# A linear-attention and gated-MLP block on one core: attention features in blocks of two heads instead of four

## The chip, the cores and the metric

The kernel runs on one core of a Trainium2 chip. The metric is the device time of one execution in microseconds (us); lower is better. Engines are named TensorE (PE; its weight loads are PEld), VectorE (DVE), ScalarE (ACT), GpSimd (POOL) and SyncE (SP, which here issues nearly all transfers).

## The reference

One transformer block over 2048 tokens of width 512, all in bf16, with a conditioning vector `c` that gives six vectors of 512 for shift, scale and gate:

```
mod = silu(c) @ w_mod  ->  sa, ca, ga, sb, cb, gb
h = layernorm(x) * (1 + ca) + sa
x = x + ga * A(h)
h = layernorm(x) * (1 + cb) + sb
x = x + gb * B(h)

A(h):  32 heads of 16; q, k, v = h @ wqkv
  pq = q @ w_phi[head];  pk = k @ w_phi[head]                  # 16 x 16 per head
  phi_q = [softmax(pq), softmax(-pq)];  phi_k likewise         # 32 features per head
  kv[f, d] = sum over tokens of phi_k[f] * v[d];  z[f] = sum over tokens of phi_k[f]
  o = (phi_q @ kv) / (phi_q . z + 1e-6);  return o @ wo
B(h):  (sigmoid(h @ w_gate) * (h @ w_up)) @ w_down            # inner width 1376
```

## The kernel before

Tokens lie in 16 tiles of 128. Everything is a task of a graph (`G.add`), with the engine that runs it, what it reads and writes, and the buffers it holds; buffers are taken from small pools, among them the 8 banks of PSUM. A text, `ORDER`, names all tasks in one sequence, and each engine runs its own tasks in that sequence; a name with `@A`, `@D` or `@P` is put on ScalarE, VectorE or GpSimd. So the sequence fixes the program of every engine and every queue, and the times in `G.add` do nothing when the kernel runs.

The stages overlap:

- Start: `warm0` (six matmuls on zeros) and `warm1_0` to `warm1_11` (one each) are matmuls whose results nobody reads. `c1`, `c2`, `c3` make silu(c); `modc...` make the modulation columns. `w_phi` is folded into the q and k weights: `bd` builds a block-diagonal matrix from `w_phi` (L578), `tpw`/`wTc` or `wqT` transpose the weights, `fold`/`foldc` multiply (L675).
- Per tile: `st1`, `rs1`, `nmr1`, `xn1` normalise, `tph` (or a transposing transfer `xT1`) transposes, `hm1` modulates into `h1T`. `K`, `V`, `Q` are projections of four matmuls of 512 columns each.
- Features (`feature_tasks`, L763 and on): `e` takes exp of both signs on ScalarE, `n` sums over the 16 features of a head on VectorE, `r` takes the reciprocal, `phi` multiplies. The 1024 features of a token stand in eight groups of 128. In a group come four heads: the order within is sign, feature, head, with the head innermost.
- `kv` (L279 to L287): for each token tile and group, one matmul with 128 features of the group as weights and the group's four heads' values with a column of ones (4 x 17 = 68 columns) as moving operand, summed over all 16 token tiles in two banks `kvacc`. A head's own sums are then one quarter of the block; `kvn` and `kvz` (L289) multiply by a mask (`mask4`) that zeroes the other heads' parts, into `kvb`.
- Queries: `qe`, `qn`, `qphi` as above, and `pT` transposes the features through a transfer. `num` (L325): four matmuls of 68 columns for each half of the groups, contracting 128 features with `kvb`; `rd` takes the reciprocal of the denominators, `u` multiplies. `oT` transposes the result, `out` multiplies by `wo`, `x1` adds the residual.
- MLP: `st2` to `xnT` and `mod` prepare the second normalised input in chunks of 1, 1, 2, 4, 4, 4 tiles; `g`, `u` with a chunk and block number are the gate and up projections, `tg` tanh, `hm` the product, `y` the down projection, `fin` the residual, `st` the store. For the last 96 rows of the inner width, in chunks of four tiles, the up projection is packed (L452): 64 weight columns a matmul, two of them side by side on the two halves of the output partitions.

In the order, key sums and projections of queries and values are interleaved, and from the numerators on, `g`, `u` and `y` matmuls stand between the attention's.

Of the kernel before, what the change touches and what calls it, by code (L numbers as in the profile page):

```python
# [23 lines left out]
HC = 4 * VC  # L24
# [15 lines left out]
pmem ld_x0b wdz warm0 c1 warm1_0 warm1_1 bd st1_2 st1_3 warm1_2 warm1_3 c2 rs1_2 ld_x0a ld_wk0 warm1_4 tpw0 st1_0 rs1_0 wTc0 st1_1 ld_wk1 rs1_1 c3 xn1_0  # L40
nmr1_1 nmr1_2 ld_x1b st1_6 st1_7 tpw1 tpw3 wTc3 wTc1 tpw2 fold10 foldc10 wTc2 ld_wm00b ld_x1a ld_wm00a tph00 fold11 fold13 rs1_4 foldc13 fold12 foldc12 xn1_3
xn1_2 xn1_1 modc1.0 tph10 tph11 st1_4 tph20 tph01 ld_x2b foldc11 tph22 warm1_5 modc1c0 hm1_11@A nmr1_4 xn1_6 xn1_7 st1_5 rs1_3@P st1_11 st1_10 warm1_6
hm1_20@A hm1_10@A tph21 warm1_7 tph41 tph42 hm1_21 rs1_6@P nmr1_3 tph13 ld_wm01a ld_wm01b modc1.1 hm1_01@A hm1_00@A hm1_41@A tph03 tph23 K2a ld_x2a tph02
modc1c1 st1_8 ld_x3a warm1_8 K1a hm1_23 xn1_5 xn1_4 tph12 nmr1_6 st1_9 hm1_03@A hm1_13@A hm1_02@A ld_wv0 wqT3 xn1_10 xn1_11 rs1_5@P K0a K0b tph31 hm1_42@A
warm1_9 hm1_12@A hm1_22@A tph32 e0.0 K3a tph30 K3b hm1_30@A ld_wmga K1b tph33 warm1_10 tph40 st1_14 st1_15 st1_13 hm1_31@A hm1_32 wqT0 e3.0 wqT1 K2b hm1_40
nmr1_5 rs1_8@P n0.0 nmr1_8 hm1_33 e2.0 V0a V1a fold03 xn1_9 xn1_8 V1b V0b e1.0 n2.0 V2a V2b tph50 hm1_50 warm1_11 xn1_15 xn1_14 n1.0 V3a wqT2 fold00 fold01
tph43 r0.0@A va1 va0 phi0.0 foldc03 fold02 foldc01 foldc02 n3.0 st1_12 foldc00 xT1_10 xT1_11 r2.0 va2@D ld_wmm2 modca.0 modca.1 hm1_60@P hm1_63@P hm1_62@P
# [12 lines left out]
hm0.4 hm0.9 u0.2 u0.0 num6a tg0.5 tg0.0 rd3a u3a u0.5 g0.2 hm0.0 hm0.5 rd6a nmr2_1 qe10.0 tg0.2 oT4 g0.10 u0.10 wd6 hm0.2 g0.3 pT7 tg0.3 u6a g0.6 num6b u0.3  # L60
y0.0 y0.1 rd6b tg0.10 hm0.10 hm0.3 num5a num5b u6b rd5b wd3 wd4 wd5 oT3 oT6 xn2_1 qe13.0 tg0.6 rd5a y0.2 u5b g0.7 tg0.7 out4 u5a oT5 qn11.0 u0.6 u0.7 xnT1
num7a hm0.6 hm0.7 mod13@A mod12@A rd7a x1_4 y0.3 out3 qphi11.1@P qphi11.0@P x1_3 st2_3 out6 mod10@A mod11@A g1.2 tg1.2 g1.1 tg1.1 num7b wd7 u1.3 u1.2 hm1.2
u7a g1.4 u1.1 y0.4 rd7b hm1.1 u1.4 y0.5 tg1.4 hm1.4 g1.0 g1.10 u1.10 g1.3 u7b st2_2 rs2_2 tg1.10 tg1.3 hm1.10 hm1.3 pT11 out5 tg1.0 u1.7 g1.7 x1_6 nmr2_2 u1.0
hm1.0 g1.5 u1.5 x1_5 qn10.0 wd8 y0.6 g1.6 oT7 xn2_2 xn2_3 g1.8 y0.7 Q14 y0.8 wd10 tg1.7 tg1.5 hm1.5 out7 u1.8 u1.6 st2_4 tg1.6 xnT2 xnT3 wd9 x1_7 qphi10.0 Q12
hm1.7 st2_6 mod21@P mod20@P qphi10.1@P y1.0 pT10 tg1.8 mod22@A mod23@A hm1.6 g1.9 y1.1 y1.2 tg1.9 u1.9 y0.9 y1.3 y1.4 g2.5 y0.10 g2.6 st2_5 qe12.0 st2_7 hm1.8
qn9.0 tg2.5 qe14.0 rs2_4 hm1.9 rs2_3 nmr2_4 y1.5 u2.0 g2.1 g2.0 tg2.0 xn2_7@D hm2.0 nmr2_3 fin0 y1.6 g2.2 tg2.2 u2.6 u2.2 hm2.2 u2.1 num11b y1.7 g2.4 rd11b
u11b xn2_6@P xnT7 xnT6 u2.5 tg2.1 xn2_5 qphi9.1@P hm2.1 tg2.6 u2.8 xn2_4 hm2.5 g2.3 num11a rd11a u11a u2.9 qphi9.0@P xnT5 y1.8 xnT4 tg2.4 u2.4 hm2.4 hm2.6
tg2.3 g2.9 u2.3 hm2.3 g2.8 tg2.8 tg2.9 u2.7 mod41@P mod43@P mod32@P mod42@P mod31@P qn13.0 g2.10 hm2.8 g2.7 y1.9 num10a qn8.0 num10b y2.0 y1.10 tg2.7 hm2.7
rd10a hm2.9 qphi8.0@P u2.10 pT9 y2.1 y2.2 y2.3 y2.4 y2.5 qn14.0 num9b rd9b qphi13.0 qphi8.1@P mod30@A mod33@A tg2.10 mod40@A y2.6 y2.7 g3.3 wr qphi13.1@P
tg3.3 oT11 g3.0 u10a rd10b u10b pT8 oT10 hm2.10 qn15.0 g3.8 num9a rd9a u9a u3.0 out11 y2.8 g3.1 y2.9 qphi14.1 fin1 x1_11 u9b u3.3 hm3.3 st1 tg3.8 tg3.0 u3.8  # L70
num8a st2_11 num8b rd8b rd8a u8a pT13 qphi15.0 hm3.8 u8b u3.9 g3.4 u3.2 out10 x1_10 qphi14.0 oT8 oT9 hm3.0 st2_10 y2.10 g3.6 u3.6 qn12.0 rs2_6 out8 tg3.4
# [89 lines left out]
def kernel(  # L161
# [102 lines left out]
    def bank(name, shape=None, dtype=FP32):  # L264
        return Buf("bank", shape or [P, 512], dtype, name)
# [793 lines left out]
```

## Time and profile before

| | us |
|---|---|
| median of 3 runs | 205.52 |
| lowest and highest | 205.25, 206.58 |
| the profiled execution | 205.02 |
| its span, first to last instruction | 203.3 |
| busy: PE, PEld | 194.9, 106.7 |
| busy: DVE, ACT, POOL | 160.6, 105.9, 102.1 |

The profile shows one execution. The end of a matmul is modelled and matmuls overlap, so a row's duration (379 ns for 512 columns) is longer than the distance between two starts; distances of starts tell what a matmul holds. A row of the timeline joins equal instructions that follow each other ("x8") and gives the first start and the stretch they cover. In rows of groups, the columns are line, engine, operation, tiles, rows*columns of the weights, shape and count, then busy us, mean ns of one, and the engine's idle time before them with what ended it. L numbers are lines of the kernel before.

### The profile page before, as it was taken

What the parts mean: (1) busy time and instruction counts of PE and PEld (TensorE: products, weight loads), DVE (VectorE), ACT (ScalarE), POOL (GpSimd) and SP (SyncE); (2) the same over time, 40 slices, a digit from 0 to 9 for tenths busy, and PEclk for the clock granted to TensorE, in tenths of its full rate; (3) what the DMA queues carried; (4) which work ended last, traced back from release to release, by engine and by line L of the source; (5) the groups of instructions that cost most, each with busy time, mean ns of one, the idle gap of its engine ahead of it and who ended that gap; (6) DMA issues with size and microseconds to landing.
All of it is one profiled execution on the core that took longest, in us unless ns stands there. A gap on an engine that the chain in (4) does not pass through costs nothing.

```text
span 203.3 us, 4138 instructions
## 1 busy us (share of the span) xinstructions
PE 194.9 (96%) x1447; PEld 106.7 (52%) x1471; DVE 160.6 (79%) x374; ACT 105.9 (52%) x257; POOL 102.1 (50%) x143
## 2 busy tenths in 40 slices
PE   7789999999999999999999999999999999999993
PEld 2455655555464687668844444444444444444442
DVE  3899999999999999999897797794969844326633
ACT  2799999999978984556451115212113311324100
POOL 4698977789689999767670056230030324000000
PEclk9999999999999999999999999999999999999999
DMA  5999975669952792417637224433112030100111
GB/s 172 331 329 182 233 264 102 123 82 280 400 213 43 146 102 55 94 37 106 125 59 103 51 54 103 101 83 77 26 26 69 13 79 31 40 13 7 50 55 55
DMA packets 49453, 22.94 MB, mean 113 GB/s; under 512 B 38065, under 2 KB 47634, under 8 KB 49426
## 3 DMA queue, kind: packets, MB, share of 16 engines
q1 hardware_dynamic: 48896, 22.59, 48.6%
q8 instruction: 13, 0.21, 0.4%
q14 instruction: 14, 0.11, 0.2%
q10 hardware_dynamic: 530, 0.02, 0.1%
HBM read 11.58 MB, written 2.10 MB: 67 GB/s over the span
## 4 chain that ended last, share of the span: by engine, by line
PE 75%; DVE 8%; ACT 4%; DMA 4%; issue 4%; POOL 3%; SPq 0%; POOLq 0%; DVEq 0%
PE y_ps L485 19%; PE u_ps L447 18%; PE g_ps L447 17%; PE a_ps L356 5%; DMA wmod_sb<-in_w_mod_dram 4%; PE k_ps L817 3%; PE warm L600 3%; DVE ks L780 3%; PE num L326 2%; POOL phi L787 2%; PE q_ps L871 2%; PE v_ps L821 2%; PE g_ps L449 1%; ACT h1T L751 1%; DVE qks L780 1%
## 5 line engine op out<-in xcount | busy, mean ns | idle before, releaser
L457 ACT ACTIVATE tg<-g_ps 128x512 bf16<-128x512 f32 (+5 forms) x66 | 28.8, 455 | 66.7 <-PE g_ps L447 39.5
L468 DVE SCALAR_TENSOR_TENSOR wmod_sb<-tg,u_ps 128x512 bf16<-128x512 bf16 (+4 forms) x63 | 30.3, 492 | 18.0 <-ACT tg L457 11.3
L485 PE MATMUL y_ps<-wd_sb,wmod_sb 128*128 128x512 bf16 (+4 forms) x180 | 44.2, 366 | 0.2
L447 PEld LDWEIGHTS <-wg_sb 128*128 128x128 bf16 (+1 forms) x252 | 21.9, 99 | 16.1 <-issue 0.2
L447 PEld LDWEIGHTS <-wu_sb 128*128 128x128 bf16 (+1 forms) x252 | 21.8, 99 | 16.0 <-issue 0.3
L784 POOL TENSOR_TENSOR qphi<-qe,qks 128x512 bf16<-128x512 bf16 x24 | 25.1, 1063 | 3.9 <-DMA pT<-qphi 1.0
L485 PEld LDWEIGHTS <-wmod_sb 128*128 128x128 bf16 (+1 forms) x187 | 17.1, 98 | 16.0 <-issue 0.6
L447 PE MATMUL u_ps<-wT_sb,wu_sb 128*128 128x512 bf16 (+2 forms) x124 | 23.8, 322 | 0.1
L447 PE MATMUL g_ps<-wT_sb,wg_sb 128*128 128x512 bf16 (+2 forms) x122 | 23.0, 321 | 0.2
L447 PE MATMUL g_ps<-wqk_sb,wg_sb 128*128 128x128 bf16 (+4 forms) x127 | 19.9, 286 | 0.1
L447 PE MATMUL u_ps<-wqk_sb,wu_sb 128*128 128x128 bf16 (+4 forms) x127 | 19.8, 286 | 0.2
L492 DVE TENSOR_TENSOR ot<-y_ps,x 128x512 bf16<-128x512 f32 (+2 forms) x17 | 11.1, 654 | 10.5 <-PE y_ps L485 10.4
L780 DVE TENSOR_REDUCE qks<-qe 128x64 bf16<-128x1024 bf16 x16 | 19.2, 1204 | 0.0
L780 DVE TENSOR_REDUCE ks<-e 128x64 f32<-128x1024 bf16 (+2 forms) x22 | 19.1, 905 | 0.0
L376 POOL TENSOR_SCALAR ve<-mv 128x2 f32<-128x2 f32 (+1 forms) x8 | 1.8, 226 | 34.2 <-DVE mv L366 34.1
L776 ACT ACTIVATE e<-k_ps 128x512 bf16<-128x512 f32 (+2 forms) x44 | 17.7, 504 | 0.1
L776 ACT ACTIVATE qe<-q_ps 128x512 bf16<-128x512 f32 x32 | 17.3, 608 | 0.8 <-POOL phi L787 0.4
L787 POOL TENSOR_TENSOR phi<-e,kr 128x1024 bf16<-128x1024 bf16 (+2 forms) x10 | 14.5, 1454 | 3.9 <-ACT kr L795 2.1
L817 PE MATMUL k_ps<-wqk_f,h1T 128*128 128x512 bf16 x61 | 15.9, 379 | 0.1
L356 PE MATMUL a_ps<-wo_sb,oT 128*128 128x512 bf16 x60 | 15.9, 379 | 0.2
L871 PE MATMUL q_ps<-wqk_f,h1T 128*128 128x512 bf16 x60 | 15.7, 379 | 0.2
L821 PE MATMUL v_ps<-wv_sb,h1T 128*128 128x512 bf16 x62 | 15.5, 379 | 0.0
(131 smaller groups left out, 306.4 us busy)
## 6 DMA issues: line engine op xcount, KB each, us to landing
out_dram<-ot SPq DMA_DIRECT2D x15, 128.0 KB, 1.8
x_sb<-in_A_x_dram SPq DMA_DIRECT2D x6, 256.0 KB, 4.9
wmod_sb<-in_w_mod_dram SPq DMA_DIRECT2D x1, 1536.0 KB, 7.4
wu_sb<-in_B_w_up_dram SPq DMA_DIRECT2D x1, 1376.0 KB, 11.0
wg_sb<-in_B_w_gate_dram SPq DMA_DIRECT2D x1, 1376.0 KB, 10.4
wd_sb<-in_B_w_down_dram SPq DMA_DIRECT2D x1, 1280.0 KB, 8.0
wmod_sb<-in_w_mod_dram SPq DMA_DIRECT2D x4, 256.0 KB, 6.0
wqk_sb<-in_A_wqkv_dram SPq DMA_DIRECT2D x2, 256.0 KB, 4.5
```

The costliest lines, as they stand in the source:

```text
L356: pe.matmul(ap_[:], lhsT=oT[:, j, :], rhs=wo_sb[:, j, :], start=(j == 0), stop=(j == KT - 1))
L447: pe.matmul(ps[:fsz, 0:n], lhsT=w[:, j, ft * P:ft * P + fsz], rhs=h[:, j, 0:n], start=(j == 0), stop=(j == KT - 1))
L457: G.add(f"tg{k}.{ft}", {"ACT": 0.13 + n * 0.00083}, lambda e, tg=tg, g_ps=g_ps, fsz=fsz, n=n: act.activation(tg[:fsz, 0:n], g_ps[:fsz, 0:n ...
L468: dve.scalar_tensor_tensor(hm_all[:fsz, hm[k].slot, ft, 0:n], tg[:fsz, 0:n], 1.0, u_ps[:fsz, 0:n], op0=ALU.add, op1=ALU.mult)
L485: mm = pe.matmul(y[:, 0:c1 - c0], lhsT=hm_all[:fsz, hm[k].slot, ft, tl * P:(tl + 1) * P], rhs=wd_sb[:fsz, ft, c0:c1], start=(ft == 0), sto ...
L776: act.activation(ee[:, a:b, s].rearrange("p g f h -> p g (f h)"), kp[:, a * 64:b * 64].rearrange("p (g n) -> p g n", n=64), ACT.Exp, scale ...
L780: dve.tensor_reduce(ks[:, a:b].rearrange("p g s h -> p (g s) h"), ee[:, a:b].rearrange("p g s f h -> p (g s) h f"), axis=AX.X, op=ALU.add)
L784: engine(e).tensor_tensor(ph[:].rearrange("p (g s f h) -> p g s f h", s=2, f=DH, h=4)[:, :, s], ee[:, :, s], ks[:, :, 1 - s].unsqueeze(2). ...
L787: engine(e).tensor_tensor(ph[:, a * P:b * P].rearrange("p (g f h) -> p g f h", f=DH, h=4), ee[:, a:b].rearrange("p g s f h -> p (g s) f h" ...
L817: pe.matmul(kp[:], lhsT=h1T[:, j, t * P:(t + 1) * P], rhs=wqk_f[:, j, D:2 * D], start=(j == 0), stop=(j == KT - 1))
L821: pe.matmul(vp[:], lhsT=h1T[:, j, t * P:(t + 1) * P], rhs=wv_sb[:, j, :], start=(j == 0), stop=(j == KT - 1))
L871: pe.matmul(qp[:], lhsT=h1T[:, j, t * P:(t + 1) * P], rhs=wqk_f[:, j, 0:D], start=(j == 0), stop=(j == KT - 1))
```

## The change

The features' layout is changed from blocks of four heads to blocks of two. A group of 128 features now holds two blocks of 64 (two heads each), each with order sign, feature, head.

- Key sums: for each group two matmuls instead of one, each with 64 weight columns and 2 x 17 = 34 moving columns, into the upper and lower 64 partitions of the same bank columns.
- Numerators: for each group two matmuls, each with 64 of the 128 rows as contraction and 34 columns, into two different banks. One task `num` now makes both halves of a tile (16 matmuls) before either `rd` may begin; a half is now every second pair of heads instead of the first or last 16 heads.
- `kvb`, `mask4` and the masking steps are half as wide; `bd` is built in four instructions instead of two; exp, sums and products of the features have innermost runs of two heads.
- `ORDER` is another sequence altogether, with other places for loads, fillers and engines.

```
-HC = 4 * VC
+HC = 2 * VC
...
-                    pe.matmul(acc[g // 4][:, (g % 4) * HC:(g % 4 + 1) * HC], lhsT=ph[:, g * P:(g + 1) * P],
-                              rhs=vaug[va.slot][:, 4 * g:4 * g + 4, :].rearrange("p h d -> p (h d)"),
-                              start=(t == 0 and g % 4 == 0), stop=(t == NT - 1), skip_group_check=True)
+                    for x in range(2):
+                        pe.matmul(acc[g // 4][64 * x:64 * x + 64, (g % 4) * HC:(g % 4 + 1) * HC], lhsT=ph[:, g * P + 64 * x:g * P + 64 * x + 64],
+                                  rhs=vaug[va.slot][:, 4 * g + 2 * x:4 * g + 2 * x + 2, :].rearrange("p h d -> p (h d)"),
+                                  start=(t == 0 and g % 4 == 0), stop=(t == NT - 1), skip_group_check=True)
...
                 dve.tensor_tensor(kvb[:, 4 * i:4 * i + 4, :].rearrange("p g (h c) -> p g h c", c=VC)[:, :, :, 0:DH],
-                                  src[:, 0:4 * HC].rearrange("p (g h c) -> p g h c", h=4, c=VC)[:, :, :, 0:DH],
-                                  mask4[:].unsqueeze(1).unsqueeze(3).to_broadcast([P, 4, 4, DH]), op=ALU.mult)
+                                  src[:, 0:4 * HC].rearrange("p (g h c) -> p g h c", h=2, c=VC)[:, :, :, 0:DH],
+                                  mask4[:].unsqueeze(1).unsqueeze(3).to_broadcast([P, 4, 2, DH]), op=ALU.mult)
...
+                nps = [bank("num") for _ in range(2)]
+
+                def f_num(e, t=t, nps=nps):
+                    for g in range(NG):
+                        for x in range(2):
+                            pe.matmul(nps[x][:, g * HC:(g + 1) * HC], lhsT=pT[t][64 * x:64 * x + 64, g, :], rhs=kvb[64 * x:64 * x + 64, g, :], start=True, stop=True)
...
-                        for g in range(4):
-                            pe.matmul(ps[:, g * HC:(g + 1) * HC], lhsT=pT[t][:, 4 * i + g, :], rhs=kvb[:, 4 * i + g, :], start=True, stop=True)
...
                     def f_u(e, i=i, ps=ps, den=den, o=o):
-                        dve.tensor_tensor(o[:, 256 * i:256 * i + 256].rearrange("p (g h d) -> p g h d", h=4, d=DH),
+                        dve.tensor_tensor(o[:].rearrange("p (g x h d) -> p g x h d", x=2, h=2, d=DH)[:, :, i],
...
-        for g in range(2):
-            pool.tensor_tensor(bd[:, :, 64 * g:64 * g + 64].rearrange("p k (f h) -> p k f h", h=4), wp_sb[:].unsqueeze(3).to_broadcast([P, KT, DH, 4]),
+        for g in range(4):
+            pool.tensor_tensor(bd[:, :, 32 * g:32 * g + 32].rearrange("p k (f h) -> p k f h", h=2), wp_sb[:].unsqueeze(3).to_broadcast([P, KT, DH, 2]),
...
-        ee = Buf("r2k", [P, NG, 2, DH, 4], BF16, q + "e")
+        ee = Buf("r2k", [P, 2 * NG, 2, DH, 2], BF16, q + "e")
...
-                    engine(e).tensor_tensor(ph[:, a * P:b * P].rearrange("p (g f h) -> p g f h", f=DH, h=4), ee[:, a:b].rearrange("p g s f h -> p (g s) f h"),
-                                            kr[:, a:b].rearrange("p g s h -> p (g s) h").unsqueeze(2).to_broadcast([P, 2 * (b - a), DH, 4]), op=ALU.mult)
+                    engine(e).tensor_tensor(ph[:, a * P:b * P].rearrange("p (g f h) -> p g f h", f=DH, h=2), ee[:, 2 * a:2 * b].rearrange("p g s f h -> p (g s) f h"),
+                                            kr[:, 2 * a:2 * b].rearrange("p g s h -> p (g s) h").unsqueeze(2).to_broadcast([P, 4 * (b - a), DH, 2]), op=ALU.mult)
```

The new order begins as below; then the stretches with the last key sums and the first numerators (`num8a` stands for both halves of tile 8).

```
+wdz warm0 pmem c1 warm1_0 warm1_1 ld_x0b c2 st1_2 st1_3 rs1_2@P ld_x0a ld_wk1 ld_x1a ld_wk0 tpw3 wTc3 st1_1 rs1_1 tpw2 bd ld_x1b ld_wm00b ld_wm00a tpw1 wTc2
+wTc1 c3 nmr1_2 st1_0 xn1_2@A st1_5 xn1_3 rs1_0@P st1_4 st1_7 nmr1_1 ld_x2b xn1_0 st1_6 fold13 fold12 tpw0 wTc0 tph21 fold11 rs1_3@P xn1_1 modc1.0 rs1_4@P
...
+r11.6 V12 V11 K13 warm1_7 K12 ld_wd ld_wg0 grb ld_wu0 r14.0 n11.4 va10 e15.4 va11 mask4 r11.4 n10.0 n15.0 phi11.2@D kv8.0 r10.0@A phi11.4@D warm1_8 kv9.0
+warm1_9 V14 e13.4 e13.0 phi10.0@D n13.4 phi11.6 wo1 e12.0 phi11.0 n13.0 phi14.0 kv10.0 V15 kv11.4 phi14.4@D r13.4@A phi13.4 va14 Q6 V13 Q5 r13.0@A phi13.0
+n12.0 n15.4 r15.0 r15.4 va12 r12.0@A qe6.0 phi12.0@D kv11.6 kv11.0 kv11.2 phi15.0@D warm1_10 phi15.4 va13 qn6.0 Q3 va15 kv12.0 kv13.4 kv13.0 kv14.0 kv15.0
+kv14.4 kv15.4 Q7 kvn0 kvz0 qe3.0 wo0 wo3 wo2 kvz1 kvn1 qphi6.1@P warm1_11 ld_wd2 num0a qphi6.0@P qn3.0 qe5.0 rd0a num2a num1a Q8 rd0b u0a u0b tpo0 qe7.0 rd2a
```

More of the change, by code (lines that the diff above doesn't have):

```diff
@@ L44 @@
[L44 to L47, printed above, removed]
@@ L186 @@
     bmask = cst.tile([P, P], BF16, name="bmask")
-    mask4 = cst.tile([P, 4], BF16, name="mask4")
+    mask4 = cst.tile([P, 2], BF16, name="mask4")
     modc = cst.tile([P, 16], FP32, name="modc")
@@ L589, in f_mask @@
     def f_mask(e):
-        with nc.allow_low_precision(reason="sums of one 1 and 31 zeros"):
-            dve.tensor_reduce(mask4[:], ident[:].rearrange("p (f h) -> p h f", h=4), axis=AX.X, op=ALU.add)
+        with nc.allow_low_precision(reason="sums of one 1 and 63 zeros"):
+            dve.tensor_reduce(mask4[:], ident[:].rearrange("p (f h) -> p h f", h=2), axis=AX.X, op=ALU.add)
     G.add("mask4", {"DVE": 0.2}, f_mask, w=["mask4"])
```

118 lines of the change are left out of this document (57 added, 61 removed).

## The prediction

> **What bounds the kernel now.** I read the page first (busy time by engine, slices, chain), then the busy time by stage, then single matmuls in the timeline of TensorE.
>
> ```profile
> PE 194.9 (96%) x1447; PEld 106.7 (52%) x1471; DVE 160.6 (79%) x374; ACT 105.9 (52%) x257; POOL 102.1 (50%) x143
> PE   7789999999999999999999999999999999999993
> PE 75%; DVE 8%; ACT 4%; DMA 4%; issue 4%; POOL 3%; SPq 0%; POOLq 0%; DVEq 0%
> ...
> core 0: us, PE busy (x) PEld busy (x) DVE busy (x) ACT busy (x) POOL busy (x), PEclk, DMA share, GB/s
> 0.00:15.00 15.00, 11.76 (x103) 6.31 (x105) 10.95 (x36) 10.22 (x29) 9.91 (x31) 1.00 0.95 277
> 15.00:30.00 15.00, 14.62 (x143) 8.44 (x144) 14.59 (x33) 14.84 (x37) 12.95 (x20) 1.00 1.10 235
> 30.00:58.00 28.00, 27.79 (x251) 15.18 (x253) 27.19 (x50) 26.73 (x78) 21.96 (x21) 1.00 0.78 209
> 58.00:70.00 12.00, 11.39 (x104) 6.48 (x103) 11.82 (x33) 10.35 (x22) 11.84 (x12) 1.00 0.38 83
> 70.00:130.00 60.00, 59.56 (x507) 37.92 (x514) 52.95 (x137) 27.72 (x67) 36.37 (x47) 1.00 0.50 84
> 130.00:200.00 70.00, 69.63 (x357) 32.38 (x362) 42.76 (x89) 16.08 (x28) 9.11 (x16) 1.00 0.18 45
> ```
>
> The reader is to see that TensorE has no room left. From 15 us to 200 us it idles 0.38 + 0.21 + 0.61 + 0.44 + 0.37 = 2.0 us in all; the only large hole is the start. The chain gives VectorE 8% of the span, but where it does so TensorE stays full beside it, with value and query projections that nobody needs yet (27.79 of 28 us between 30 and 58 us). So work added to TensorE after 15 us moves the end almost one for one, and at most those 2.0 us can swallow any of it. The profiled execution took 205.02 us (span 203.3 us and 1.7 us around it); the runs shown have a median of 205.52 us, 0.5 us above it. The sum is made against 205.0, and 0.5 is added at the end.
>
> **The price of the small matmuls.** The change touches two groups:
>
> ```profile
> L326 PE MATMUL num<-kvb,pT 128*128 128x68 bf16 x128 | 8.0, 194 | 0.4 <-DVE kvb L299 0.4
> L282 PE MATMUL kvacc<-vaug,phi 128*128 128x68 bf16 x128 | 6.0, 194 | 0.1
> ...
> 32.27 0.42 PE L282 MATMUL kvacc<-vaug,phi 128*128 128x68 bf16 x8
> 32.53 0.27 PE L744 MATMUL tp_h<-ident,xn 128*128 128x128 bf16 x2
> ...
> 10.30 0.55 PE L630 MATMUL modc_ps<-sc_bf,wmod_sb 128*128 128x1 bf16 x16
> L630 PE MATMUL modc_ps<-sc_bf,wmod_sb 128*128 128x1 bf16 x32 | 1.1, 164 | 0.0
> ```
>
> Eight key-sum matmuls of one token tile hold TensorE from 32.27 to 32.53: 0.26 us, 32 ns each. (Durations overlap, so only starts count.) Numerators have the same shape. 256 such matmuls: 32 x 0.26 = 8.3 us. What can halving the columns give? Sixteen matmuls with one single column take 0.55 us, and without the last one's 0.164 us that is 0.386 / 15 = 26 ns each. So one full-array matmul with its own weight load hardly gets below 26 ns at any width, and 68 columns already stand at 32. A gain can come only from two half-array matmuls running side by side.
>
> Column tiles of 64 already stand in this kernel (the packed up-projection, L452), so their pairs have rows:
>
> ```profile
> 128.38 0.38 PE L485 MATMUL y_ps<-wd_sb,wmod_sb 128*128 128x512 bf16 x1
> 128.69 0.30 PE L452 MATMUL u_ps<-wT_sb,wu_sb 128*64 128x256 bf16 x2
> ...
> 128.69 0.63 PE L452 MATMUL u_ps<-wT_sb,wu_sb 128*64 128x256 bf16 x8
> 129.25 0.39 PE L485 MATMUL y_ps<-wd_sb,wmod_sb 128*128 128x512 bf16 x1
> 129.47 0.81 PE L449 MATMUL g_ps<-wT_sb,wr_sb 128*128 128x512 bf16 x3
> ...
> 91.21 0.60 PE L447 MATMUL u_ps<-wqk_sb,wu_sb 128*128 128x256 bf16 x4
> 91.65 0.60 PE L447 MATMUL g_ps<-wqk_sb,wg_sb 128*128 128x256 bf16 x4
> ...
> 128.68 0.14 PEld L452 LDWEIGHTS <-wu_sb 128*64 128x64 bf16 x4 [0.43 <-issue]
> L452 PEld LDWEIGHTS <-wu_sb 128*64 128x64 bf16 x24 | 1.1, 109 | 1.3 <-issue 1.3
> ```
>
> Two packed matmuls of 256 columns together take 0.30 us, about one's duration, so a pair does run side by side. But the visit costs. From the y matmul at 128.38 to the g matmul at 129.47 are 1.09 us. In it lie two 512-column matmuls (129.47 - 129.25 = 0.22 each) and four pairs of 256 columns (91.21 to 91.65: 0.44 for four). 1.09 - 0.44 - 0.44 leaves **0.21 us per visit**: 128.38 to 128.69 is 0.31 where 0.22 is usual (0.09 on the way in), and 128.69 to 129.25 is 0.56 where four pairs need 0.44 (0.12 on the way out). The weight loads stop too ("0.43 <-issue"). I call this the toll of a visit: it looks as if the array ran empty before its tiling is changed, once on either side.
>
> **How many visits.** In the new order, TensorE's tasks between which no other form stands are, for the key sums: 0; 1 and 2; 3; 4; 5; 6; 7; 8; 9; 10; first part of 11; its other parts; 12 to 15 together: **13 visits**. For the numerators: 0, 2, 1 together; 4; 3; 6 and 5; 7; 11; 10; 8; 9; 15; 14; 13; 12: **13 visits**. Key sums never stand next to numerators. Before, all of these were full-array matmuls, without a toll.
>
> Toll: 26 x 0.21 = **+5.5 us**. For row tiles (numerators) the nearest row is the tiny K = 1 product at the start, still at the slow clock:
>
> ```profile
> 3.92 0.26 PE L569 MATMUL c_ps<-ones,c_row 1*128 1x1 bf16 x4
> 4.11 2.31 PE L600 MATMUL warm<-wd_sb 128*128 128x512 bf16 x5
> L569 PE MATMUL c_ps<-ones,c_row 1*128 1x1 bf16 x4 | 0.3, 165 | 0.0
> ```
>
> The last of the four starts at 3.92 + 0.26 - 0.165 = 4.02, the next full matmul at 4.11: 0.09 us instead of 0.03, so at least 0.06 us on the way out. Bounds for a row visit: 0.06 and 0.21; I take 0.21, since a column visit is nearest in size and clock. At the low end 13 x 0.15 = 2.0 us less. The Trainium skill, TensorEngine Tiling (Array Packing), Key Properties, says that changing the tiling mode, not just the tile, drains TensorE; by that rule row tiles pay like column tiles, 5.5 us in all, where the K = 1 row alone would allow 3.5.
>
> Pairs: four weight loads of 64 columns span 0.14 us and one takes 0.109, so the second pair starts 0.03 us behind the first. A pair of 34 columns streams in less (0.11 us for 256 columns is 0.43 ns a column: 15 ns), so the load sets it: 0.03 us, eight pairs 0.24 us against 0.26. 32 x 0.02 = **-0.6 us**. Bounds: 17 ns a pair, were loads hidden (256 x 0.017 = 4.4, a gain of 3.9); 52 ns, were each of the two to need the 26 ns of the single-column row (13.3, a loss of 5.0). I stay at the load row, which has the very shape of the key sums.
>
> **The other edits.** Masking of the key sums halves in elements:
>
> ```profile
> L294 DVE TENSOR_TENSOR kvb<-kvacc,mask 128x256 bf16<-128x256 f32 x2 | 0.8, 423 | 0.0
> L580 POOL TENSOR_TENSOR bd<-wp_sb,bmask 128x256 bf16<-128x256 bf16 x2 | 1.5, 770 | 2.1 <-DMA wp_sb<-in_A_w_phi_dram 2.1
> 14.78 0.38 PE L600 MATMUL warm<-wd_sb 128*128 128x512 bf16 x1
> ...
> 22.31 0.38 PE L600 MATMUL warm<-wd_sb 128*128 128x512 bf16 x1
> 7.53 0.40 PE L679 MATMUL fold_ps<-bd,wT_sb 128*128 128x128 bf16 x4
> 14.20 0.38 PE L817 MATMUL k_ps<-wqk_f,h1T 128*128 128x512 bf16 x1
> L787 DVE TENSOR_TENSOR phi<-e,kr 128x1024 bf16<-128x1024 bf16 x7 | 4.7, 682 | 0.3 <-POOL h1T L753 0.3
> ```
>
> The two masking steps lose at most half of 0.423 us each, 0.3 us of VectorE together, which TensorE's own lateness hides: 0. Reciprocals, products and feature steps keep their counts and elements; only their innermost runs get shorter, from 4 elements to 2. Bounds: 0, and for the feature products on VectorE twice their time, of which the seven key products here are 4.7 us. They run at 0.67 ns an element with runs of 4, quicker than any step that goes element by element (the mask, 423 / 256 = 1.65 ns), so two elements at a time are enough for them; I take 0. The reciprocal of a tile's first half waits for sixteen numerator matmuls instead of four, about 0.12 us a tile, under the gate and up matmuls: 0; uncovered it would be 16 x 0.12 = 1.9 us.
>
> Fillers: both orders hold the 18 "warm" matmuls. In the old one four start after the first key projection at 14.20, from 14.78 to 22.31; in the new order nine do (warm1_3 to warm1_11, five of them among the last key sums). Five more at 0.22 us, where TensorE is full: **+1.1 us**; 0 if TensorE happens to wait there.
>
> Start: bd becomes four instructions on GpSimd, between 1.5 us (by elements) and 3.1 us (by instructions); I take 2.0. It now also stands behind rs1_2. The folds need it, and the first fold started at 7.53 in a stretch where TensorE was waiting anyway for the modulation weights (10.30). Of the 0.5 to 2.5 us that it is later, I let 0.4 us reach the first key projection: **+0.4 us** (0 to 1.5). SyncE's queue keeps its eight leading loads, in another order among them: 0. But the value weights (wv0) now stand behind the transposing loads wqT2 and wqT3:
>
> ```profile
> 9.42 1.01 SPq L551 DMA_DIRECT2D wv_sb<-in_A_wqkv_dram  x1
> 10.47 1.78 SPq L669 DMA_TRANSPOSE wT_sb<-in_A_wqkv_dram  x1
> wv_sb<-in_A_wqkv_dram SPq DMA_DIRECT2D x1, 512.0 KB, 7.0
> 19.38 1.03 PE L821 MATMUL v_ps<-wv_sb,h1T 128*128 128x512 bf16 x4
> ```
>
> Each of the two holds the queue for 1.78 us: 9.42 + 3.6 = 13.0, and 7.0 us to landing make 20.0. The new order has the first value projection behind those of the keys of five tiles (K1 to K4 and K0, 0.86 us each), so at about 14.6 + 4.3 = 18.9 and the transposes between them: 0, at most 0.6.
>
> Sum: 5.5 - 0.6 + 1.1 + 0.4 = 6.4 us. Of the 2.0 us of idle time I let 0.5 be filled by it: 5.9 us. 205.0 + 5.9 + 0.5 = **211.4 us**.
>
> **Rivals.** (a) The two halves do not run side by side when they are so short: 52 ns a pair, 22 ns over my 30: 256 x 0.022 = 5.6 us, 217.0. For it: no row shows a pair this short, and 26 ns was what a single column took. Against it: the packed loads start in pairs. Chance 0.12. The Trainium skill, TensorEngine Tiling (Array Packing), Instruction Overhead, gives each matmul about 60 cycles however few its columns, and warns against taking the tiling factor from a dimension that is already small; the 26 ns row agrees with the floor, and by that rule this rival is the rule rather than the exception.
>
> (b) TensorE stays at half its clock through the start. The fillers of the first 6 us start 0.43 us apart (five from 4.11 until 6.24, when the key weights' transposes follow) and later matmuls of that width 0.22; the new order puts two instead of five behind c1, so TensorE stands idle from about 5.0 until the key weights land at 6.2. If the fast clock then comes only after another 4.7 us of dense work, half of that is lost: +2.3 us, 213.7. For it: the fast clock came only after 5 us without a gap. Against it: the start has holes that may hide it. Chance 0.12.
>
> (c) The tolls vanish in holes: the new order leaves TensorE waiting for VectorE toward the end of the key sums, where five fillers now stand, and the tolls fall into that wait. For it: VectorE is as full as TensorE there (27.19 of 28). Half of the tolls, the fillers and the later start hidden: 211.4 - 2.8 - 1.1 - 0.4 = 207.1; with the cheap row visits (2.0 less) 205.1. Against it: the window has 0.21 us of idle time on TensorE, and the tolls of thirteen visits put TensorE behind VectorE. Chance 0.12.
>
> (d) Faster: the visits are free, because a matmul of 34 columns leaves so little in the array that emptying it costs nothing, and the pairs stream at 17 ns with their loads hidden. The place is every visit, the price 205.5 - 3.9 + 1.1 + 0.4 = 203.1 us; it decides from a toll below 0.015 us a visit, since 26 of that use up what lies between 203.1 and 203.5. For it: the pair row, side by side. Against it: the K = 1 row, where single columns still pay 0.06 us on the way out. Chance 0.06.
>
> **How the numbers follow.** The forecast, 211.4, has 0.58, with 209.4 to 213 as its own range (cheap row visits below; above, the rest of the start's 1.5 us and the 0.5 of idle time left unfilled). About 1% (2 us) is what a measurement of this kernel tells from no change. Slower by over 1%: forecast, (a) and (b), 0.58 + 0.12 + 0.12 = 0.82. Within 1%: (c), 0.12. Faster by over 1%: (d), 0.06. The range 207.0 to 217.5 holds the forecast, (a), (b) and the upper end of (c), and leaves out (d) and the rest of (c).
>
> **What would show it.** In the changed profile: kvacc groups as 128*64 and num groups as 64*128, x256 each, pairs starting within some ns and 0.03 us apart; gaps of about 0.1 us in the starts on both sides of every visit; TensorE still full from 15 us on, the numerators beginning 3 to 4 us later than at 58.57; fillers between 45 and 62 us. Wrong would be: pairs 0.05 us apart (a), 427 ns matmuls after 7 us (b), TensorE idle by several us before the first numerators (c), or starts without gaps around the visits (d).

## The result: 212.3 us, 3% slower, and the profile after

The changed kernel takes 212.26 us (median of 4 runs, 211.67 to 212.38) against 205.38 us of the kernel before beside it: a ratio of 1.0305, 95% interval 1.0264 to 1.0345. The prediction was 211.4 us, range 207.0 to 217.5.

The page of the changed kernel: its span, its busy times and the granted clock of TensorE by slices of a fortieth:

```profile
span 209.8 us, 4656 instructions
PE 199.9 (95%) x1699; PEld 106.7 (51%) x1727; DVE 163.1 (78%) x383; ACT 107.5 (51%) x250; POOL 99.8 (48%) x140
...
PEclk9859999999999999999999999999999999999999
```

Its busy time by stage (the columns are those of the prediction's table; PEclk is the third figure from the end):

```profile
0.00:15.00 15.00, 10.95 (x94) 6.50 (x96) 10.66 (x36) 8.86 (x22) 11.34 (x38) 0.78 0.99 249
15.00:30.00 15.00, 14.68 (x125) 8.18 (x126) 14.46 (x36) 14.80 (x36) 13.20 (x16) 0.99 0.99 257
30.00:60.00 30.00, 29.68 (x343) 14.95 (x343) 28.10 (x48) 27.77 (x78) 21.90 (x21) 1.00 0.74 203
60.00:73.00 13.00, 12.49 (x186) 6.67 (x189) 11.63 (x32) 10.16 (x20) 11.36 (x11) 1.00 0.40 61
```

TensorE is as full as before from 15 us on; the span is 6.5 us longer. The numerators begin at 63.28 us, 4.7 us later than in the kernel before. New is the clock: 0.78 in the first 15 us, where the kernel before had 1.00. PEclk has to be read with care here, since it counts the time until the clock first comes up as full speed. In the kernel before, the first 128-column transposes still start 107 ns apart and only from 6.9 us on 56 ns apart, though PEclk says 1.00 for all of it. From then on that kernel keeps the fast clock; the changed kernel has it from 5.0 us, but runs at half speed again from 8.5 to 15.3 us.

The groups of the two tiled matmuls in the changed kernel:

```profile
L282 PE MATMUL kvacc<-vaug,phi 128*64 128x34 bf16 x256 | 6.3, 185 | 0.0
L325 PE MATMUL num<-kvb,pT 64*128 64x34 bf16 x256 | 5.4, 175 | 0.0
```

One visit of each in the timeline (start, length, operation, shape and count):

```profile
33.33 0.38 PE L819 MATMUL k_ps<-wqk_f,h1T 128*128 128x512 bf16 x1
33.64 0.24 PE L282 MATMUL kvacc<-vaug,phi 128*64 128x34 bf16 x4
33.64 0.43 PE L282 MATMUL kvacc<-vaug,phi 128*64 128x34 bf16 x16
34.00 0.61 PE L819 MATMUL k_ps<-wqk_f,h1T 128*128 128x512 bf16 x2
...
112.63 0.38 PE L487 MATMUL y_ps<-wd_sb,wmod_sb 128*128 128x512 bf16 x1
112.95 0.37 PE L325 MATMUL num<-kvb,pT 64*128 64x34 bf16 x16
113.25 0.82 PE L449 MATMUL u_ps<-wT_sb,wu_sb 128*128 128x512 bf16 x2
```

A visit of the key sums: from the last full matmul's start at 33.33 to the next full one at 34.00 are 0.67 us; less the 0.22 us of a 512-column matmul, TensorE is held for 0.45 us, where the same eight groups took 0.26 us before (0.455 and 0.257 in the unrounded starts). On the way in stand 0.31 instead of 0.22 (0.09 us lost). Sixteen matmuls span 0.43 us with the last one's 0.185: 0.43 - 0.185 = 0.245 for seven pairs and a second partner, 0.03 us a pair and a little more. That leaves 0.45 - 0.245 - 0.09 = 0.115 us on the way out. A visit of the numerators: 112.63 to 113.25 is 0.62, less 0.22 is 0.40 us; in it 0.32 - 0.22 = 0.10 on the way in, 0.37 - 0.175 = 0.195 for the sixteen (25 to 27 ns a pair) and 0.105 out.

So pairs do run side by side, as short as they are. A visit of one tile costs 0.20 us more than before for key sums (0.455 against 0.257) and 0.14 us for numerators (0.394 against 0.257). The expectations below were written with 0.21 and 0.15. Each further tile in the same visit takes 0.25 us for key sums, as before, and 0.20 instead of 0.25 us for numerators, so that a visit of the numerators of two tiles is 0.08 us dearer than with full-array matmuls (0.594 against 0.511) and one of three tiles 0.03 us (0.797 against 0.767).

### The profile page after: what moved, and what is told of

The parts are those of the page before. It is cut to its first block, busy times and chain, and to the rows that moved or that the text cites. A ratio compares the mean times of both kernels' runs of the same rounds, so it can differ in the third digit from the quotient of the medians.

```text
span 209.8 us, 4656 instructions
## 1 busy us (share of the span) xinstructions
PE 199.9 (95%) x1699; PEld 106.7 (51%) x1727; DVE 163.1 (78%) x383; ACT 107.5 (51%) x250; POOL 99.8 (48%) x140
## 4 chain that ended last, share of the span: by engine, by line
PE 88%; DVE 5%; POOL 2%; DMA 1%; issue 1%; ACT 1%; POOLq 0%
PE y_ps L487 18%; PE g_ps L449 17%; PE u_ps L449 17%; PE v_ps L823 7%; PE k_ps L819 6%; PE a_ps L358 5%; PE q_ps L873 5%; PE kvacc L282 3%; PE tp_h L746 2%; PE num L325 2%; DMA x_sb<-in_A_x_dram 1%; PE warm L602 1%; PE g_ps L451 1%; DVE st L704 1%; PE modc_ps L618 1%
## 5 line engine op out<-in xcount | busy, mean ns | idle before, releaser
L459 ACT ACTIVATE tg<-g_ps 128x512 bf16<-128x512 f32 (+4 forms) x66 | 29.1, 456 | 66.2 <-PE g_ps L449 47.2
L487 PE MATMUL y_ps<-wd_sb,wmod_sb 128*128 128x512 bf16 (+4 forms) x184 | 44.8, 366 | 0.2 <-issue 0.2
L449 PEld LDWEIGHTS <-wg_sb 128*128 128x128 bf16 (+1 forms) x252 | 21.4, 99 | 16.5 <-issue 1.2
L449 PEld LDWEIGHTS <-wu_sb 128*128 128x128 bf16 (+1 forms) x252 | 21.4, 99 | 15.6 <-issue 0.4
L786 POOL TENSOR_TENSOR qphi<-qe,qks 128x512 bf16<-128x512 bf16 x23 | 24.0, 1062 | 9.0 <-DVE qks L782 7.2
L487 PEld LDWEIGHTS <-wmod_sb 128*128 128x128 bf16 (+1 forms) x187 | 17.6, 98 | 18.9 <-DVE wmod_sb L470 0.3
L449 PE MATMUL u_ps<-wT_sb,wu_sb 128*128 128x512 bf16 (+2 forms) x120 | 23.0, 321 | 0.2
L789 POOL TENSOR_TENSOR phi<-e,kr 128x1024 bf16<-128x1024 bf16 (+2 forms) x12 | 17.1, 1428 | 7.0 <-DVE phi L789 4.2
L449 PE MATMUL g_ps<-wqk_sb,wg_sb 128*128 128x128 bf16 (+4 forms) x127 | 19.3, 287 | 0.2
L823 PE MATMUL v_ps<-wv_sb,h1T 128*128 128x512 bf16 x60 | 16.0, 380 | 0.2
L873 PE MATMUL q_ps<-wqk_f,h1T 128*128 128x512 bf16 x57 | 15.6, 379 | 0.3
```

Source lines behind the costliest of these rows:

```text
L449: pe.matmul(ps[:fsz, 0:n], lhsT=w[:, j, ft * P:ft * P + fsz], rhs=h[:, j, 0:n], start=(j == 0), stop=(j == KT - 1))
L459: G.add(f"tg{k}.{ft}", {"ACT": 0.13 + n * 0.00083}, lambda e, tg=tg, g_ps=g_ps, fsz=fsz, n=n: act.activation(tg[:fsz, 0:n], g_ps[:fsz, 0:n ...
L487: mm = pe.matmul(y[:, 0:c1 - c0], lhsT=hm_all[:fsz, hm[k].slot, ft, tl * P:(tl + 1) * P], rhs=wd_sb[:fsz, ft, c0:c1], start=(ft == 0), sto ...
L786: engine(e).tensor_tensor(ph[:].rearrange("p (g s f h) -> p g s f h", s=2, f=DH, h=2)[:, :, s], ee[:, :, s], ks[:, :, 1 - s].unsqueeze(2). ...
L789: engine(e).tensor_tensor(ph[:, a * P:b * P].rearrange("p (g f h) -> p g f h", f=DH, h=2), ee[:, 2 * a:2 * b].rearrange("p g s f h -> p (g ...
L823: pe.matmul(vp[:], lhsT=h1T[:, j, t * P:(t + 1) * P], rhs=wv_sb[:, j, :], start=(j == 0), stop=(j == KT - 1))
```

## Experiments

**The order alone.** The new `ORDER` put into the kernel before; each numerator's second half behind its first:

```
-num0a qphi6.0@P qn3.0 ...
+num0a num0b qphi6.0@P qn3.0 ...
```

> The kernel before, with its features in blocks of four heads and full-array key sums and numerators, but with the new order (each numerator's second half stands right behind its first). Theory T (the visits to the tiled mode cost 0.21 us for key sums and 0.15 us for numerators, the late fillers 1.1 us): the 26 visits, 4.4 us, are gone and the fillers stay, 207.9 us. Rival O (the new order costs it all): about 212. Rival L (the layout's other edits cost it: shorter runs on VectorE, GpSimd and ScalarE): about 205.5.

Measured: 209.93 us (208.43 to 210.91), ratio 1.0197 (1.0114 to 1.028). Without one tiled matmul more than before, the new order alone loses more than half of the difference. That was 2 us over theory T and well over rival L. The busy time by stage of this run, with PEclk the third figure from the end:

```profile
7.00:15.00 8.00, 6.75 (x74) 5.26 (x75) 7.30 (x24) 6.82 (x19) 7.66 (x14) 0.53 1.16 281
15.00:18.00 3.00, 3.00 (x15) 1.55 (x14) 2.04 (x8) 1.87 (x5) 2.45 (x5) 0.55 1.18 324
18.00:30.00 12.00, 11.95 (x96) 6.60 (x94) 11.54 (x24) 11.94 (x29) 10.30 (x12) 1.00 0.95 240
```

TensorE ran at half its clock from about 7 to 17.7 us, into the first key projections. In the changed kernel's own profile it was 8.5 to 15.3 us. Its key sums of tile 10 also wait 0.53 us for VectorE's features, which they do not in the changed kernel.

**The start with fillers.** The same kernel, five late fillers out, ten put into the holes of the start (here with "warm" for the renumbered names):

```
-c1 warm1_0 warm1_1 ld_x0b ... tpw2 bd ... fold12 tpw0 wTc0 tph21 ... modc1.0 ...
+c1 warm1_0 warm1_1 warm warm warm ld_x0b ... tpw2 warm warm warm warm bd ... fold12 warm tpw0 wTc0 tph21 warm ... modc1.0 warm ...
...
-K13 warm1_7 K12 ... kv8.0 ... warm1_8 kv9.0 warm1_9 ... warm1_10 ... warm1_11
+K13 K12 ... kv8.0 ... kv9.0 ...
```

> The new order with full-array matmuls (as in the run with the order alone, 209.9 us), the five late fillers taken out and ten put into the holes of the start: three behind the two after c1, four behind the second transpose of the key weights, one each behind the second fold, the first tile's transposes and the first modulation product. Theory K (the start runs at half clock until 15 to 17.7 us since TensorE has holes there): fast clock from about 7 us on, 1.5 to 2.5 us less, 207.5 to 208.4. If the start's clock does not matter: 209.5 to 209.9.

Measured: 206.33 us (206.00 to 206.78, 10 runs), ratio 1.0026 (1.0004 to 1.0049). That is 3.6 us less than the order alone, more than theory K had asked for. The clock in the same windows:

```profile
7.00:15.00 8.00, 6.75 (x90) 4.46 (x88) 7.66 (x25) 7.54 (x21) 7.61 (x15) 1.00 1.19 281
15.00:18.00 3.00, 3.00 (x20) 1.43 (x18) 2.93 (x9) 3.00 (x8) 2.73 (x5) 1.00 1.17 324
```

The two profiles show where it went: 1.7 us up to the first key sums (30.91 against 29.18 us), 1.5 us from there to the first numerator, where the five late fillers stood, and 0.6 us after it. So the clock of the start is about half of the 3.6 us, not all of it. What is left of the new order, 206.3 against 205.7 us, is small. The spread also fell from 2.5 us to 0.8 us. That a run's time depends on when its clock comes up would fit this, but it is not shown: only one run of each kernel has a profile.

**The changed kernel with that start.** The same edit in the changed kernel; taking out the filler between tiles 8 and 9 joins two visits of key sums:

```
-... kv8.0 ... warm1_8 kv9.0 ...
+... kv8.0 ... kv9.0 ...
 (and the start as in the run above)
```

> The changed kernel with the fillers of the run with the new order and a warm start: five late ones out, ten into the holes of the start. 12 visits of key sums, 13 of numerators. Theory T (tolls one for one on top of the same order): 206.3 + 12 x 0.21 + 13 x 0.15 = 210.8 us. Rival W (part of the tolls falls into waits of this order, as the 2.3 us between the order alone and the changed kernel suggest): 208.7. Rival L (the layout's other edits cost as well): over 211.5.

Measured: 210.34 us (209.87 to 210.63), ratio 1.0225 (1.019 to 1.0261): 1.9 us less than the changed kernel, and **4.0 us over the same order and start with full-array matmuls**. Both profiles show a clock of 1.00 from 7 us on. The two visits that were shown above for the changed kernel, in the run with full-array matmuls, the new order and the warm start:

```profile
32.21 0.59 PE L817 MATMUL k_ps<-wqk_f,h1T 128*128 128x512 bf16 x2
32.64 0.42 PE L282 MATMUL kvacc<-vaug,phi 128*128 128x68 bf16 x8
32.90 0.59 PE L817 MATMUL k_ps<-wqk_f,h1T 128*128 128x512 bf16 x2
...
108.47 0.38 PE L485 MATMUL y_ps<-wd_sb,wmod_sb 128*128 128x512 bf16 x1
108.69 0.42 PE L326 MATMUL num<-kvb,pT 128*128 128x68 bf16 x8
108.94 0.59 PE L447 MATMUL u_ps<-wT_sb,wu_sb 128*128 128x512 bf16 x2
```

With the starts of both profiles, the 12 visits of key sums cost 0.198 us more each, eleven visits of numerators 0.137 each, and the two with two and three tiles 0.08 and 0.03: 2.4 + 1.5 + 0.1 = 4.0 us. The tolls arrive whole, and the 4.5 us that the expectation counted were 0.5 too many. Theory T holds, and rival L has nothing left to explain. The 2.3 us between the order alone and the changed kernel were less than 4.0 because the order alone lost 1.2 us more before its first key sums (30.91 against 29.75 us), and, as rival W has it, because a wait ahead of the key sums of tile 10 took up about 0.5.

**Key sums put off, so that fewer visits remain.** On top of that kernel:

```
-kv0.0 ... kv1.0 kv2.0
+kv0.0 kv1.0 kv2.0
(likewise kv6.0 before kv7.0, kv8.0 before kv9.0, kv11.4 before kv11.6)
```

> The changed kernel with the warm start (210.3 us) and only the key sums put off (tile 0's to 1's, 6's to 7's, 8's to 9's, the first part of 11's to the others), the numerators where they were: 9 visits of key sums instead of 12, 13 of numerators. Theory T: 3 x 0.21 = 0.6 us less, and up to 0.8 more less if the wait of 0.78 us before tile 10's key sums goes with them, as it went in the run with all visits merged: 209.7 to 208.9. If merging gains nothing or the matmuls alone set the price: 210.3 or more.

Measured: 208.94 us (208.54 to 210.36), ratio 1.0186 (1.0116 to 1.0256): 1.4 us less, of which 0.6 are three tolls and the rest the wait ahead of tile 10. The intervals of the two ratios overlap, so this rests on the two profiles: the visits of key sums, with the waits ahead of them, hold TensorE for 1.4 us less. The kernel with the warm start, then the one with fewer visits:

```profile
53.25 0.38 PE L823 MATMUL v_ps<-wv_sb,h1T 128*128 128x512 bf16 x1
54.34 0.43 PE L282 MATMUL kvacc<-vaug,phi 128*64 128x34 bf16 x16 [0.71 <-DVE phi L789]
```

```profile
51.52 0.68 PE L282 MATMUL kvacc<-vaug,phi 128*64 128x34 bf16 x32
52.13 1.04 PE L823 MATMUL v_ps<-wv_sb,h1T 128*128 128x512 bf16 x4
53.10 0.43 PE L282 MATMUL kvacc<-vaug,phi 128*64 128x34 bf16 x16
```

Two tiles in one visit (51.52 to 52.13) take 0.61 us, against twice 0.36 and 0.09 for a second way in.

**Key sums and numerators put off.** As above, and numerators joined too (3 with 6 and 5, 11 with 10, 8 with 9, 15, 14 and 13):

> That kernel with some key sums and numerators put off until they stand next to the following ones: 9 visits of key sums instead of 12 and 8 of numerators instead of 13, the matmuls the same. Theory T: 3 x 0.21 + 5 x 0.15 = 1.4 us less than the changed kernel with the warm start. Rival (the price lies in the matmuls or the layout): no less; it could be more where putting off makes somebody wait.

Measured: 212.59 us (211.25 to 212.97), 2.2 us more instead of 1.4 less. A numerator moved next to another one waits there for what it needs, and so do the matmuls behind it:

```profile
76.70 0.36 PE L325 MATMUL num<-kvb,pT 64*128 64x34 bf16 x15 [0.59 <-DVE o L336]
...
118.79 0.60 PE L449 MATMUL g_ps<-wT_sb,wg_sb 128*128 128x512 bf16 x2 [0.81 <-DVE o L336]
...
135.47 0.35 PE L325 MATMUL num<-kvb,pT 64*128 64x34 bf16 x15 [0.42 <-DVE x L363]
136.10 0.60 PE L449 MATMUL g_ps<-wT_sb,wg_sb 128*128 128x512 bf16 x2 [0.28 <-DVE o L336]
```

These four waits make 2.1 us. This profile's clock also fell back, between 14.4 and 17.8 us, and its first key sums start 1.7 us later than those of the kernel before this one (31.68 against 29.93 us), with the same order up to there. As a test of the toll of numerators its time is inconclusive. The starts are not: the joined visit of tiles 10 and 11 holds TensorE for 0.594 us, where two single ones take 0.79.

**Visits of the numerators doubled.** On the kernel with the new layout in the old order (next below), a single-column matmul in the middle of each tile's sixteen; nobody reads its result:

```
                     for g in range(NG):
+                        if g == 4:
+                            pe.matmul(nps[0][:, 400:401], lhsT=ident[:], rhs=ident[:, 0:1], start=True, stop=True)
```

> As the kernel with the new layout in the old order, with one full-array matmul of a single column, whose result nobody reads, in the middle of each tile's sixteen numerator matmuls: 16 more visits for 16 more instruction pairs. Theory T: each adds about 0.20 us (0.106 out, 0.025 + 0.096 in, less one pair's 0.025), 16 x 0.20 = 3.2 us over that kernel, 213.0. Rival N (the number of instructions costs, not the change of mode): 16 of them are worth 0.4 us, 210.2.

Measured: 215.28 us (214.81 to 215.92), 2.6 us over its base for 16 instruction pairs. Rival N, 0.4 us, falls. One of these visits:

```profile
110.16 0.27 PE L327 MATMUL num<-kvb,pT 64*128 64x34 bf16 x8
110.36 0.18 PE L325 MATMUL num<-ident 128*128 128x1 bf16 x1
110.47 0.27 PE L327 MATMUL num<-kvb,pT 64*128 64x34 bf16 x8
```

Out to the full array and back is 110.16 to 110.47, 0.31 us, where four pairs need 0.10: 0.21 us, as expected. From the first numerator to the end, where both profiles have the fast clock, it is 152.2 us against 149.3: 2.9 of the 3.2 us arrive there. The medians differ by less, 2.6 us; that runs of the base lost some time to their clock ahead of the numerators, as its profile does, would explain it.

**The layout alone.** The changed kernel with the old order, where one task makes both halves of a numerator, at the place of one of the two:

```
-... u0a num0b num4a num1b rd0b ... u2a rd4a num2b qn3.0 ... out0 num4b rd2b ...
+... u0a rd0b ... u2a qn3.0 ... out0 num4a rd4a rd2b ...
```

> The new layout and tiled matmuls in the old order, so with the old start and the old fillers; a numerator task stands where its first half stood, for tiles 3, 4, 6, 13 and 14 where the second stood. 12 visits of key sums and 13 of numerators. Theory T (visits cost 0.21 and 0.15 us, as the changed kernel's starts have it): 205.4 + 2.5 + 1.9 = 209.8 us. Rival O (the new order's start and waits cost most of it): 206 or less. Rival L (the layout's other edits): over 211.

Measured: 212.67 us (212.13 to 214.25, 6 runs), ratio 1.0335 (1.0306 to 1.0363), 2.9 us over theory T and in the place of rival L. The trace tells where, though. The one task for both halves takes two banks at a time and makes sixteen matmuls where the old order had four; the matmuls behind it wait:

```profile
78.35 0.56 PE L449 MATMUL u_ps<-wqk_sb,wu_sb 128*128 128x128 bf16 x7 [0.82 <-DVE o L336]
...
113.10 0.59 PE L449 MATMUL g_ps<-wT_sb,wg_sb 128*128 128x512 bf16 x2 [0.69 <-ACT tg L459]
```

```profile
31.50:35.00 3.50, 3.50 (x46) 1.52 (x42) 1.66 (x3) 1.97 (x6) 2.07 (x2) 0.51 0.33 66
```

The two waits are 1.5 us; neither stands in the kernel before. The second fence is its busy time in one stretch and shows half the clock from 31.5 to 35 us in the profiled execution, which was also its slowest (214.25 us). From the first numerator to the end, where this profile has the fast clock, the kernel takes 149.3 us and the kernel before 144.7: 4.6 us, where the tolls of numerators make 1.9 by theory T. So the excess lies there and not in the clock, and the two waits explain about half of it; the rest stays open. That the layout's other edits cost nothing is shown by the rows below, not by this time.

**The late fillers.** Five out of the changed kernel, and the same five moved behind c1:

```
-r11.6 V12 V11 K13 warm1_7 K12 ... warm1_8 kv9.0 warm1_9 V14 ... warm1_10 ... warm1_11
+r11.6 V12 V11 K13 K12 ... kv9.0 V14 ...
```

> The changed kernel without the five fillers among and after the last key sums. Theory T: 5 x 0.22 us, and 0.21 more because two visits of key sums become one (the filler between tiles 8 and 9 goes): 212.3 - 1.3 = 211.0 us. Rival (c) of the prediction, that TensorE would be waiting there anyway: 212.3.

> The same five fillers moved to the start, behind the two that follow c1, so that seven stand there as long as the key weights are on their way. If the slow clock between 8.5 and 15.3 us costs nothing: as with the fillers out, 211.0 us. If it costs (rival b): clock fast from 7 us on and up to 2 us less, 209 to 210.5.

Measured: 212.2 us (the middle of three runs, 211.65 to 212.6; a fourth took 260.86 us, for a reason that no profile shows) and 211.9 us (210.74 to 212.01). Taking the fillers out gained nothing that the times can tell. Where three of them stood, TensorE now waits ahead of the key sums of tile 10 (profile of the kernel without them):

```profile
54.19 1.04 PE L823 MATMUL v_ps<-wv_sb,h1T 128*128 128x512 bf16 x4
55.94 0.43 PE L282 MATMUL kvacc<-vaug,phi 128*64 128x34 bf16 x16 [0.71 <-DVE phi L789]
```

And its clock came up only at 17.3 us: until then its first key projections start 0.43 us apart, though the mean granted clock of this execution is given as 1.00. The first key sums are 0.9 us later for it (30.70 against 29.75 us). From the first key sums to the first numerator it takes 32.8 us where the changed kernel takes 33.5: 0.7 us of the expected 1.3 are gained there. Seven fillers behind c1 did not hold the clock either: it was fast from 6.6 to 13.4 us and half from there to 16.8. The ten fillers in the later holes held it in three of the four profiles that have them; in the fourth (key sums and numerators put off) it fell back all the same.

**The kernel before without its four fillers behind the first key projection, and with seven in the holes of its start:**

```
-... warm1_8 K1a ... warm1_9 hm1_12@A ... warm1_10 tph40 ... warm1_11 xn1_15 ...
+... K1a ... hm1_12@A ... tph40 ... xn1_15 ...
 (second kernel also:  tph00 +3, fold13 +1, fold12 +1, modc1.0 +1, tph11 +1)
```

> The kernel before without the four fillers that stand behind the first key projection. If TensorE is full there: 4 x 0.22 us less, 204.5. If they stand in waits, as most of the five late ones of the new order seem to: 205.4. If they keep the clock up: slower than 205.4.

> The kernel before, untouched in layout, without its four fillers behind the first key projection and with seven in the holes of its start (three behind the first tile's first transpose, one each behind two folds, the first modulation product and the second transpose of tile 1). If its clock too falls back in some runs between 10 and 16 us: 204.0 to 205.0 us and a narrower spread. If it never does: 205.1, as with the four fillers out.

Measured: 205.13 us, ratio 0.9976 (0.9957 to 0.9995), and 205.32 us, ratio 0.9981 (0.995 to 1.0011). The first is faster than the kernel before by a hair, a quarter of a per cent, though its profile has half the clock from 12.2 to 15.6 us. The second is not told apart from the kernel before; its spread is no narrower. So in the median the old start has next to nothing to gain from fillers, and it is the new order's start that lacks them. The kernel before loses its clock too in some runs: of the 23 beside the first of these two, four with a mean granted clock of 0.983 took 206.5 to 206.7 us, and eight with 1.000 took 204.7 to 205.7 us.

## Why the prediction was right

- **TensorE is the bound, extra work moves the end.** Right: the 4.0 us that the starts show for the tolls arrive whole where clock and order are the same, and 2.9 of 3.2 us where visits were added. The prediction let 0.5 us be hidden; next to nothing was.
- **The toll, 0.21 us a visit, read from three packed visits of another matmul.** Right within 0.02 us: a visit pays 0.20 us beside what its tiles need, for column tiles (0.455 us less 0.253 for one tile more) and for row tiles (0.394 less 0.200). Of the bounds 0.06 and 0.21 for row tiles the upper one holds. The rule of the Trainium skill (TensorEngine Tiling (Array Packing), Key Properties) that a change of mode drains TensorE agrees: row tiles pay the 0.20 us that column tiles pay.
- **The pairs, -0.6 us.** The eight pairs of a tile were to take 0.24 instead of 0.26 us. Column tiles gain nothing (0.253 against 0.254 us), and row tiles gain nearly three times as much (0.200). Tolls and pairs together are 13 x 0.198 + 1.6 = 4.2 us in the changed kernel, forecast 5.5 - 0.6 = 4.9.
- **Rival (a), 52 ns a pair.** Wrong: 25 to 32 ns. If each of the two halves paid the about 60 cycles that the Trainium skill gives for every matmul (TensorEngine Tiling (Array Packing), Instruction Overhead), a pair would need twice the 26 ns of the single-column row, 52; the rows show that two half-array matmuls share what one full one needs.
- **Late fillers, +1.1 us.** Too dear: without them the way from the first key sums to the first numerator is 0.7 us shorter, of which 0.2 are the visit that went with them. They stood partly in a wait of 0.7 us for VectorE's features. Here rival (c) was right in its place.
- **The start, +0.4 us, and rival (b).** The size came out, but not for its reason, and that is luck. The first key projection starts at 14.57 instead of 14.20 us. With the warm start, where `bd` is as late and the clock is fast from 5.1 us on, it starts at 14.19, so it was not `bd` that cost it. What cost it is rival (b) in part, the half clock from 8.5 to 15.3 us in the profiled execution; I gave it 0.12. By the first key sums it is 0.7 us (29.75 against 29.09). The other three runs have a mean granted clock of 1.000, which tells nothing of a late rise. The start and the late fillers together cost 1.9 us in the changed kernel (212.3 to 210.3), where 1.5 were forecast. My term for GpSimd was close: the four pieces of `bd` took 1.6 us, not the 2.0 of the estimate.
- **The order itself, no term.** The prediction priced the new order by its fillers, its start and its visits alone. With full-array matmuls and a warm start it still takes 0.7 us more than the old one (206.3 against 205.7); which waits these are stays open.
- **The other edits, 0.** Right. The rows of the changed kernel are those of before, within 0.03 us for the sums and for the products of features of 512 and 1024 elements, and 0.29 instead of 0.42 for the masks. (Half of 0.423 twice is 0.42, not the 0.3 us of the prediction; the masks lost 0.27, and the term is 0 either way.)

```profile
L294 DVE TENSOR_TENSOR kvb<-kvacc,mask 128x128 bf16<-128x128 f32 x2 | 0.6, 288 | 1.0 <-PE kvacc L282 1.0
L789 DVE TENSOR_TENSOR phi<-e,kr 128x1024 bf16<-128x1024 bf16 x6 | 4.2, 705 | 1.2 <-ACT e L778 1.2
L582 POOL TENSOR_TENSOR bd<-wp_sb,bmask 128x128 bf16<-128x128 bf16 x4 | 1.6, 418 | 0.0
```

The sum: tolls 4.0 us, 0.7 for what the new order costs with full matmuls and a warm start, 1.9 for start and late fillers (the one visit that goes with them included): 6.6 of the measured 6.9 us. The forecast had 4.9, nothing, and 1.5, less 0.5 hidden. So the mechanism and the main term were right. That the total came within 0.9 us is also luck: tolls and fillers 1.3 us too dear stand against an order, a start and idle time that were 1.5 us too cheap.

## What to carry to other kernels

Count the visits, not the matmuls: a visit from full-array to tiled matmuls and back costs TensorE about 0.2 us in this kernel, so tiling pays only where more is saved in one visit. Matmuls of 68 columns, at 30 ns already near the 26 ns of a single column, have little to give: nothing as column tiles, and 0.06 us a token tile as row tiles. A visit of three tiles of numerators is still 0.03 us dearer than with full-array matmuls, so the numerators would pay from four tiles a visit on; this is an estimate from those rows, and no run has such a visit. A profile that holds even one tiled visit has the price in it: compare the starts on both sides with those of ordinary neighbours. When a whole order is replaced, look at the granted clock of the start first, and compare kernels only with the same clock there.

## What I had not expected of the hardware

- The fast clock is lost again while TensorE works with holes, none of them longer than 1.5 us: in the changed kernel fast from 5.0 to 8.5 us, half to 15.3, fast to the end (its longest hole is 1.48 us, from 6.66 to 8.14). In the kernel with the layout alone it is at half once more for 3.4 us from 31.5 us, after holes of at most 0.33 us but 48 single-column matmuls. Once the clock has come up, the stretches at one speed that end before the last change last 3.4 us or two, three or five times that in all these profiles. What share of work holds the clock no run shows.
- Pairs of row tiles with 128 weight columns each start 25 ns apart, quicker than pairs of column tiles with 64 (32 ns).
